# Attention blocks and product tiles of the later chunks moved to other steps, a few gate tiles' quadratic kept in PSUM

## The chip, the cores and the metric

The kernel runs on one core of one Trainium2 chip. The metric is the device time of one execution, in microseconds. Smaller is better.

## The reference

A gated linear attention feeds a network with a rational gate (the first network), and that feeds four experts (the second network). All data is float32.

```python
f = 1.0 / (1.0 + np.exp(-f_logit))              # B=4, H=8, S=768, D=48
for t in range(S):
    state = f[:, :, t, :, None] * state + np.einsum('bhd,bhe->bhde', k[:, :, t], v[:, :, t])
    y[:, :, t] = np.einsum('bhd,bhde->bhe', q[:, :, t], state)
x = y as (3072 tokens, 384)

h = x @ w_in                                    # 384 -> 2048
P = a[0] + a[1] * h + a[2] * h * h + a[3] * h * h * h
Q = 1.0 + np.abs(b[0]) * np.abs(h) + np.abs(b[1]) * h * h
x = (P / (Q + 1e-06)) @ w_out                   # 2048 -> 384

p = domain_probs / (domain_probs.sum(-1, keepdims=True) + 1e-09)
for e in range(4):
    out += p[:, e:e + 1] * (np.maximum(x @ w1[e], 0.0) @ w2[e])   # 384 -> 1024 -> 384
```

## The kernel before

**Chunks, tiles and steps.** The 768 positions are cut in six chunks of 128; a chunk holds 512 tokens (four batches). For a chunk, the first network has 16 tiles of 128 hidden units (`in1` is a tile's first product, its second product is part of an `out1`), and the second has 4 experts of 8 tiles (`in2`, `out2`). Every product of these tiles is split in three float32r products of a high and a low part (`wh`, `wl`, `gh`, `gl`), nine matmuls of 128x512 for an `in1`, `in2` or `out2`. One expert tile is one step `v`, 192 in all, so a chunk of the second network lasts 32 steps. While chunk c - 1 goes through the second network in steps 32(c - 1) to 32c - 1, chunk c goes through the attention and the first network in between. Chunk 0 has the first network to itself ahead of step 0: the "fill", with plain float32 products (`fill_in`, `fill_out`) and a time `tau = v + 19`.

**The order of the products** is written out in `first_mix_steps` and `product_order`. In a step, TensorE makes `in2` of the next tile, `out2` of the last one, and where the list `at` names the step, one `in1`. The list `ends` names four steps at which four finished first-network tiles are multiplied with their second weights at once (a "group", `out1`, 36 matmuls). A group uses the same three PSUM banks `acc` as `out2`, so `evac2` (L1018) first empties them: VectorE multiplies by the probabilities into `t`, GpSimd adds `t` to `o` (L1019). `evac1` (L1034, L1036) empties the group's sums. At a group's step the next `in2` is made early. The weights come in the order in which the list uses them, 14 halves ahead on SyncE's queue. A first use (all within steps -1 to 32) is split by ScalarE (L819) and GpSimd (L820) and stored; later uses load the split form.

**The gate** of a tile (`gate_in`, `gate_step`) takes two steps. ScalarE copies `h` out of the bank and makes `q` (the square), `r` and `y` (L929 to L935); VectorE makes the polynomials and one Newton step in `q` (L944 to L958, L968, L970), ScalarE and VectorE the two parts `gh` (L960) and `gl` (L975). `relu(v)` does the same for the second network (L983, L984). Engines take their instructions in program order: a step's relu stands ahead of its gate, the evacuation behind.

**The attention** of a chunk has four blocks (one per batch). `Att.t0` gives a block's offset, and `Att.stage` says what it does in steps 1 to 6 behind it: (1) `exp`, `w` (L431), four `scans` (L438); (2) `inverse` on ScalarE, `k_hat` on GpSimd (L452), `newton1` (L457), `newton2` (L462); (3) `q_hat` on GpSimd (L467); (4) scores (L471) and `masked` (L482); (5) transposed keys and outputs (`keys_and_y`, L487, L495), `k_copy`, `x_hi`; (6) state products (L538), `x_lo` (L552), `finish` (L564, L565). `PA`, `PB`, `ACT0`, `DVE1`, `REST` are places within a step: within `in2`, within `out2`, ahead of the gate on ScalarE, behind the gate on VectorE, and at the step's end. Each block's loads of f, k, q and v are issued on SyncE's queue in steps -1, 0 and 2. Blocks of chunks 2 and later keep some of their data in banks 6 and 7; those of chunk 1 use banks 5 to 7.

**Write-out.** When a chunk is through the second network, `write_out` transposes it by batch (L1043), ScalarE copies it to one of two buffers (L1050), and SyncE sends it out (L1052). `warm` (L608) makes 128x128 products that nobody reads.

Of the kernel before, what the change touches and what calls it, by code (L numbers as in the profile page):

```python
# [24 lines left out]
NJ1 = 16  # L25
# [320 lines left out]
def first_mix_steps():  # L346
# [3 lines left out]
    for c in range(1, NCH):  # L350
        p = NE * NJ2 * (c - 1)
        if c == 1:
            at = [10, 11, 12, 13, 14, 15, 16, 17, 18, 19, 20, 21, 23, 24, 25, 26]
            ends = (16, 20, 24, 29)
        else:
            at = [2, 3, 4, 5] if c == 2 else [-1, 1, 3, 5]
            at += [7, 9, 11, 13, 15, 17, 19, 21, 23, 24, 25, 26]
            ends = (8, 16, 24, 29)
        for j, s in enumerate(at):
            when[p + s] = (c, j)  # L360
        for n, s in enumerate(ends):
            groups[p + s] = (c, n)
# [205 lines left out]
class Att:  # L568
# [17 lines left out]
    def t0(c, b):  # L586
        if c == 1:
            return -6 + 3 * b
        if c == 2:
            return (8, 14, 20, 26)[b]  # L590
        return NE * NJ2 * (c - 1) - (30, 24, 17, 9)[b]
# [86 lines left out]
    def stage(self, blk, k):  # L678
        rs = range(NP)
        if k == 1:  # L680
# [8 lines left out]
        if k == 5:  # L689
            copy = [] if blk.last else [blk.k_copy]  # L690
            return {PB: 5 * idle + [blk.keys_and_y] + 3 * idle, REST: copy + [blk.x_hi]}
        if k == 6:
# [4 lines left out]
    def begin(self, v):  # L697
        ops = tuple([] for _ in range(7))
        for c in range(1, NCH):
            for b in reversed(range(NB)):  # L700
                k = v - self.t0(c, b)
# [7 lines left out]
def fused(ctx, tc, aps, consts, gm, big, dp, prep, flag_op):  # L709
# [215 lines left out]
    def gate_in(u):  # L925
        h = u[2]
        if u[0]:
            h = gp.tile([128, 512], F32, tag="h", name="h")
            nc.scalar.copy(out=h, in_=u[2])  # L929
        q = gp.tile([128, 512], F32, tag="q", name="q", bufs=3) if u[0] else banks[5 + u[1] % 2]  # L930
        r = gp.tile([128, 512], F32, tag="r", name="r")
# [133 lines left out]
    for v in range(-FILL - 6, LAST + 1):  # L1065
# [33 lines left out]
        if v in (LAST - 4, LAST - 3):  # L1099
            for b in range(2):  # L1100
                write_out(NCH - 1, b + 2 * (v - LAST + 4), banks[6 + b])
        if 0 <= c < NCH - 1 and k == 2:
            for b in range(2):
                write_out(c, b + (2 if c else 0), banks[6 + b])
        fill_run(ops[PB], 9 * any(item[0] == "out2" for item in items), True)
# [5 lines left out]
        for item in items[lead:]:  # L1111
            if item[0] == "in2":
                emit(item)
                if v + 1 < LAST:
                    relu(v + 1)
        if 0 <= c < NCH - 1 and k == (1 if c else 2):
            for b in range(2):
                write_out(c, b + (0 if c else 2), banks[6 + b])
        for item in items[lead:]:
# [8 lines left out]
        if tau == -1:  # L1128
            spread_probs()
        if 0 <= tau - 2 < NJ1:  # L1130
            fill_out(tau - 2)
# [198 lines left out]
```

## Time and profile before

| | |
|---|---|
| median of 3 runs | 1368.79 us (1368.64 to 1369.47) |
| the profiled execution | 1367.35 us |
| its span, first to last instruction | 1365.5 us |
| TensorE busy | 1325.7 us (97%) |
| VectorE busy | 870.5 us (64%) |
| ScalarE busy | 663.1 us (49%) |
| GpSimd busy | 287.6 us (21%) |
| mean granted TensorE clock | 0.993 |

All rows come from the profiled execution, so a sum is made against its span and then set beside the median. In the rows PE is TensorE, DVE VectorE, ACT ScalarE, POOL GpSimd, SP SyncE; L984 is line 984 of the kernel; `gl<-bank,gh` names what is written and what is read, and the name behind an arrow in a wait is what the wait ended with. [...]

### The profile page before, as it was taken

The page shows a single profiled execution, that of the slowest core. Times are in us where ns is not written, and L with a number is a line of the kernel's source. Part 1 is how long each engine was busy: PE and PEld are TensorE (multiplying, and loading weights), DVE is VectorE, ACT ScalarE, POOL GpSimd, SP SyncE. Part 2 cuts the span into 40 slices and gives each one's busy share as a digit, 9 for nine tenths or more (in the row PEclk, how much of TensorE's full clock was granted, in tenths as well). Part 3 has the DMA queues.
Part 4 walks back from the last instruction along what each step waited for, and adds up shares of the span by engine and source line. Part 5 has one row for each costly group of instructions (what it writes and reads, how often), then busy time and mean ns, then how long its engine had stood idle before and what let it go on. Part 6 is the DMA issues. An engine that isn't in the chain of part 4 may idle for free.

```text
span 1365.5 us, 19581 instructions
## 1 busy us (share of the span) xinstructions
PE 1325.7 (97%) x7152; PEld 1060.7 (78%) x7152; DVE 870.5 (64%) x1367; ACT 663.1 (49%) x1152; POOL 287.6 (21%) x257
## 2 busy tenths in 40 slices
PE   7899999898899999999999999999999999999998
PEld 6444788777788888888888888888888888888887
DVE  7999659677748576757666757576575465552221
ACT  3897448666536545525545535553445453431111
POOL 0133555566420020120110111001111000111010
PEclk9999999999999999999999999999999999999999
DMA  8547877667875666667656758665657676667660
GB/s 298 199 174 260 284 259 263 223 242 254 301 255 176 207 219 189 188 207 228 221 166 204 227 166 267 198 208 186 216 176 243 191 196 195 192 192 239 195 195 28
DMA packets 115706, 291.03 MB, mean 213 GB/s; under 512 B 13105, under 2 KB 28817, under 8 KB 114833
## 3 DMA queue, kind: packets, MB, share of 16 engines
q1 hardware_dynamic: 115024, 289.51, 65.9%
q8 instruction: 59, 0.97, 0.3%
q14 instruction: 47, 0.38, 0.1%
q10 hardware_dynamic: 576, 0.18, 0.1%
HBM read 240.83 MB, written 48.81 MB: 212 GB/s over the span
## 4 chain that ended last, share of the span: by engine, by line


## 5 line engine op out<-in xcount | busy, mean ns | idle before, releaser
L863 PE MATMUL bank<-x,w 128*128 128x512 f32 x2448 | 595.1, 391 | 6.7 <-DVE gl L984 6.7
L863 PEld LDWEIGHTS bank<-x,w 128*128 128x128 f32 x2448 | 457.2, 188 | 103.9 <-DVE gl L984 8.8
L873 PE MATMUL bank<-gh,w 128*128 128x512 f32 x1584 | 495.0, 394 | 6.6 <-DVE t L1018 6.6
L873 PEld LDWEIGHTS bank<-gh,w 128*128 128x128 f32 x1584 | 295.5, 189 | 73.2 <-DVE t L1018 7.9
L873 PE MATMUL bank<-gl,w 128*128 128x512 f32 x792 | 309.8, 391 | 0.0
L984 DVE SCALAR_TENSOR_TENSOR gl<-bank,gh 128x512 fp32r<-128x512 f32 x192 | 131.4, 685 | 154.5 <-ACT gh L983 154.2
L1019 POOL TENSOR_TENSOR o<-o,t 128x512 f32<-128x512 f32 x69 | 88.9, 1317 | 529.1 <-DVE t L1018 529.1
L873 PEld LDWEIGHTS bank<-gl,w 128*128 128x128 f32 x792 | 149.3, 189 | 31.3
L983 ACT ACTIVATE gh<-bank 128x512 fp32r<-128x512 f32 x192 | 113.7, 593 | 122.6 <-PE bank L863 122.6
L949 DVE SCALAR_TENSOR_TENSOR q<-q,sc,r 128x512 f32<-128x512 f32 x80 | 61.6, 770 | 141.8 <-ACT r L934 141.8
L960 ACT CAST gh<-q 128x512 fp32r<-128x512 f32 x80 | 49.2, 615 | 186.7 <-DVE q L958 186.6
L820 POOL TENSOR_TENSOR w<-rawbuf,w 128x384 fp32r<-128x384 f32 x96 | 104.5, 1113 | 88.6 <-ACT w L819 74.2
L929 ACT COPY h<-bank 128x512 f32<-128x512 f32 x80 | 46.8, 585 | 114.6 <-PE bank L863 113.9
L1036 DVE TENSOR_TENSOR s<-s,bank 128x512 f32<-128x512 f32 x45 | 31.0, 688 | 84.5 <-PE bank L873 84.4
L975 DVE TENSOR_TENSOR gl<-q,gh 128x512 fp32r<-128x512 f32 x80 | 55.9, 699 | 33.8 <-ACT gh L960 33.6
L950 ACT ACTIVATE r<-q,sc 128x512 f32<-128x512 f32 x80 | 58.0, 725 | 25.1 <-DVE q L949 18.4
L944 DVE SCALAR_TENSOR_TENSOR q<-q,r 128x512 f32<-128x512 f32 x80 | 69.5, 868 | 0.1
L935 ACT ACTIVATE y<-h,sc 128x512 f32<-128x512 f32 x80 | 64.2, 803 | 0.0
L958 DVE SCALAR_TENSOR_TENSOR q<-y,sc,q 128x512 f32<-128x512 f32 x80 | 62.2, 778 | 1.8
L970 DVE SCALAR_TENSOR_TENSOR y<-y,sc,h 128x512 f32<-128x512 f32 x80 | 61.1, 764 | 2.8
L951 ACT ACTIVATE r<-r 128x512 f32<-128x512 f32 x96 | 60.7, 633 | 3.0
L968 DVE TENSOR_TENSOR y<-y,h 128x512 f32<-128x512 f32 x80 | 57.2, 716 | 0.0
(113 smaller groups left out, 1220.5 us busy)
## 6 DMA issues: line engine op xcount, KB each, us to landing
w<-ws SPq DMA_DIRECT2D x448, 384.0 KB, 3.6
ws<-w SPq DMA_DIRECT2D x96, 384.0 KB, 4.1
raw<-in_w_dram SPq DMA_DIRECT2D x16, 768.0 KB, 6.3
rawbuf<-in_w_dram SPq DMA_DIRECT2D x64, 192.0 KB, 3.9
v<-in_v_dram SPq DMA_DIRECT2D x24, 320.0 KB, 4.8
f<-in_qkf_dram SPq DMA_DIRECT2D x24, 256.0 KB, 4.0
k<-in_qkf_dram SPq DMA_DIRECT2D x24, 256.0 KB, 4.3
q<-in_qkf_dram SPq DMA_DIRECT2D x24, 256.0 KB, 4.6
```

Source lines behind the costliest of these rows:

```text
L820: nc.gpsimd.tensor_tensor(out=t[:, 1], in0=r, in1=t[:, 0].bitcast(F32), op=ALU.subtract)
L863: nc.tensor.matmul(ps, a[:, o], b[:, kk, :], start=(n == 0), stop=(n == 8))
L873: nc.tensor.matmul(acc[m], a[:, o], b, start=(start and n == 0), stop=(stop and n == last))
L935: nc.scalar.activation(out=y, in_=h, func=AF.Identity, scale=sc[:, 0:1], bias=sc[:, 1:2])
L944: vec.scalar_tensor_tensor(out=q0, in0=q0, scalar=QC, in1=r0, op0=ALU.add, op1=ALU.mult)
L949: vec.scalar_tensor_tensor(out=q, in0=q, scalar=sc[:, 5:6], in1=r, op0=ALU.mult, op1=ALU.add)
L951: nc.scalar.activation(out=r, in_=r, func=AF.Exp, scale=-1.0)
L958: vec.scalar_tensor_tensor(out=q0, in0=y0, scalar=sc[:, 3:4], in1=q0, op0=ALU.subtract, op1=ALU.mult)
L970: vec.scalar_tensor_tensor(out=y, in0=y, scalar=sc[:, 2:3], in1=h, op0=ALU.subtract, op1=ALU.mult)
L983: nc.scalar.activation(out=gh, in_=h, func=AF.Relu)
L984: nc.vector.scalar_tensor_tensor(out=gl, in0=h, scalar=0.0, in1=gh.bitcast(F32), op0=ALU.max, op1=ALU.subtract)
L1019: nc.gpsimd.tensor_tensor(out=o[c][:, m], in0=o[c][:, m], in1=t, op=ALU.add)
```

## The change

Five things change together. (1) Chunk 2's first-network tiles and groups take chunk 1's pattern (one tile per step from the eleventh step on), and chunk 3's first two tiles come two steps and one step later. (2) The blocks of chunk 2 start at offsets 20, 25, 30, 35 instead of 8, 14, 20, 26, and those of chunk 3 at 42, 47, 52, 57 instead of 34, 40, 47, 55; a block's last step then falls together with the next one's first, and `begin` takes the older block first. (3) The first block of chunk 1 does its first three stages a step later, with `q_hat` in the same step as `newton2`, its scores at the step's end and `masked` in the next step; ten `warm` products are put ahead of the fill's last but one `fill_out`. (4) `q` of tiles 0 to 8 of chunk 1 lies in bank 6 or 7 instead of SBUF. (5) Chunk 0's write-out uses bank 5, one batch at a time over two steps; that of chunks 1 to 4 is made wholly in its third step instead of its second and third.

```diff
--- before.py
+++ after.py
@@ -349,11 +349,11 @@
     when, groups = {}, {}
     for c in range(1, NCH):
         p = NE * NJ2 * (c - 1)
-        if c == 1:
+        if c < 3:
             at = [10, 11, 12, 13, 14, 15, 16, 17, 18, 19, 20, 21, 23, 24, 25, 26]
             ends = (16, 20, 24, 29)
         else:
-            at = [2, 3, 4, 5] if c == 2 else [-1, 1, 3, 5]
+            at = [1, 2, 3, 5] if c == 3 else [-1, 1, 3, 5]
             at += [7, 9, 11, 13, 15, 17, 19, 21, 23, 24, 25, 26]
             ends = (8, 16, 24, 29)
         for j, s in enumerate(at):
@@ -587,7 +587,9 @@
         if c == 1:
             return -6 + 3 * b
         if c == 2:
-            return (8, 14, 20, 26)[b]
+            return 20 + 5 * b
+        if c == 3:
+            return 42 + 5 * b
         return NE * NJ2 * (c - 1) - (30, 24, 17, 9)[b]
 
     def start(self, fetch):
@@ -676,7 +678,10 @@
                     self.blocks[c, b].load_v()
 
     def stage(self, blk, k):
-        rs = range(NP)
+        if blk.c == 1 and blk.b == 0 and k < 5:
+            return ({}, {ACT0: [blk.exp], DVE1: [blk.w], REST: [blk.scans]},
+                    {ACT0: [blk.inverse], POOL1: [blk.k_hat], DVE1: [blk.newton1], REST: [blk.newton2, blk.q_hat]},
+                    {REST: [blk.all_scores]})[k - 1]
         if k == 1:
             return {ACT0: [blk.exp], DVE1: [blk.w], REST: [blk.scans]}
         if k == 2:
@@ -688,7 +693,8 @@
         idle = [lambda: None]
         if k == 5:
             copy = [] if blk.last else [blk.k_copy]
-            return {PB: 5 * idle + [blk.keys_and_y] + 3 * idle, REST: copy + [blk.x_hi]}
+            first = [blk.masked] if blk.c == 1 and blk.b == 0 else []
+            return {DVE1: first, PB: 5 * idle + [blk.keys_and_y] + 3 * idle, REST: copy + [blk.x_hi]}
         if k == 6:
             upd = [] if blk.last else 4 * idle + [blk.all_updates] + 4 * idle
             return {PA: upd, DVE1: [blk.x_lo], REST: [] if blk.last else [blk.finish]}
@@ -697,7 +703,7 @@
     def begin(self, v):
         ops = tuple([] for _ in range(7))
         for c in range(1, NCH):
-            for b in reversed(range(NB)):
+            for b in reversed(range(NB)) if c == 1 else range(NB):
                 k = v - self.t0(c, b)
                 if 1 <= k <= 6:
                     for at, fs in self.stage(self.blocks[c, b], k).items():
@@ -927,7 +933,7 @@
         if u[0]:
             h = gp.tile([128, 512], F32, tag="h", name="h")
             nc.scalar.copy(out=h, in_=u[2])
-        q = gp.tile([128, 512], F32, tag="q", name="q", bufs=3) if u[0] else banks[5 + u[1] % 2]
+        q = gp.tile([128, 512], F32, tag="q", name="q", bufs=3) if u[0] > 1 or u[0] and u[1] > 8 else banks[5 + u[0] + u[1] % 2]
         r = gp.tile([128, 512], F32, tag="r", name="r")
         y = gp.tile([128, 512], F32, tag="y", name="y")
         nc.scalar.activation(out=q, in_=h, func=AF.Square)
@@ -1099,9 +1105,11 @@
         if v in (LAST - 4, LAST - 3):
             for b in range(2):
                 write_out(NCH - 1, b + 2 * (v - LAST + 4), banks[6 + b])
-        if 0 <= c < NCH - 1 and k == 2:
+        if c == 0 and k in (2, 3):
+            write_out(c, 2 * k - 4, h1)
+        if 0 < c < NCH - 1 and k == 2:
             for b in range(2):
-                write_out(c, b + (2 if c else 0), banks[6 + b])
+                write_out(c, b, banks[6 + b])
         fill_run(ops[PB], 9 * any(item[0] == "out2" for item in items), True)
         for item in items[lead:]:
             if item[0] == "out2":
@@ -1113,9 +1121,11 @@
                 emit(item)
                 if v + 1 < LAST:
                     relu(v + 1)
-        if 0 <= c < NCH - 1 and k == (1 if c else 2):
+        if c == 0 and k in (2, 3):
+            write_out(c, 2 * k - 3, h1)
+        if 0 < c < NCH - 1 and k == 2:
             for b in range(2):
-                write_out(c, b + (0 if c else 2), banks[6 + b])
+                write_out(c, b + 2, banks[6 + b])
         for item in items[lead:]:
             if item[0] == "out1":
                 emit(item)
@@ -1127,6 +1137,8 @@
                 gate[u[:2]] = gate_in(u)
         if tau == -1:
             spread_probs()
+        if tau == NJ1:
+            att.warm(10)
         if 0 <= tau - 2 < NJ1:
             fill_out(tau - 2)
         for f in ops[REST]:
```

## Rows read from the trace of the kernel before

**Rows 1.** Stretches of the span: length, each engine's busy time (instructions), granted clock, DMA.

```profile
234.10:262.80 28.70, 24.46 (x97) 19.73 (x97) 18.15 (x28) 16.83 (x33) 18.63 (x17) 0.88 0.60 202
262.80:294.10 31.30, 30.39 (x199) 24.74 (x198) 23.89 (x36) 22.03 (x43) 17.45 (x17) 1.00 0.65 229
294.10:322.80 28.70, 24.11 (x114) 18.43 (x112) 23.93 (x35) 19.51 (x35) 15.44 (x15) 1.00 0.85 301
...
340.00:376.00 36.00, 32.41 (x157) 26.04 (x155) 28.81 (x44) 19.08 (x36) 18.12 (x17) 1.00 0.87 301
376.00:561.00 185.00, 184.49 (x1067) 152.18 (x1066) 116.59 (x187) 88.43 (x150) 26.77 (x26) 1.00 0.66 209
```

**Rows 2.** TensorE's waits from 136 to 376 us: total, times, longest.

```profile
PE bank L863 <- DVE gl L984: 6.7, 5, 2.5
PE bank L873 <- DVE t L1018: 6.6, 3, 4.2
```

**Rows 3.** Stretches behind two waits, the clock as share of full speed.

```profile
242.80:249.70 6.90, 5.49 (x13) 4.39 (x14) 6.15 (x10) 2.31 (x6) 5.47 (x4) 0.51 0.00 1
...
126.00:130.20 4.20, 4.20 (x6) 1.35 (x6) 4.05 (x8) 0.63 (x1) 1.28 (x1) 0.59 1.05 400
```

**Rows 4.** TensorE's waits from 376 to 1270 us.

```profile
PE bank L1043 <- POOL o L1019: 2.2, 3, 0.8
```

**Rows 5.** VectorE's timeline ahead of step 16's evacuation: start, length, instruction.

```profile
225.43 0.55 DVE L552 TENSOR_TENSOR x<-bank,x 128x384 fp32r<-128x384 f32 x1
226.50 0.73 DVE L564 TENSOR_TENSOR am<-bank,s 48x192 f32<-48x192 f32 x2
...
235.06 1.35 DVE L438 TENSOR_TENSOR_SCAN g<-bank,sc 112x128 f32<-112x128 f32 x4
```

**Rows 6.** VectorE's groups from 195 to 345 us: count, busy us, mean ns, idle before.

```profile
L946 DVE SCALAR_TENSOR_TENSOR q<-q,r 128x512 f32<-128x512 f32 x13 | 14.1, 1085 | 0.4
L944 DVE SCALAR_TENSOR_TENSOR q<-q,r 128x512 f32<-128x512 f32 x14 | 13.8, 982 | 0.0
```

**Rows 7.** VectorE's groups from 400 to 1240 us.

```profile
L958 DVE SCALAR_TENSOR_TENSOR q<-y,sc,q 128x512 f32<-128x512 f32 x64 | 48.0, 751 | 1.7
...
L946 DVE SCALAR_TENSOR_TENSOR q<-q,r 128x512 f32<-128x512 f32 x15 | 10.4, 692 | 0.5
```

**Rows 8.** Groups of the whole span: the same product with a bank.

```profile
L944 DVE SCALAR_TENSOR_TENSOR bank<-bank,r 128x512 f32<-128x512 f32 x16 | 11.1, 692 | 0.1
```

**Rows 9.** GpSimd's groups from 195 to 345 us.

```profile
L820 POOL TENSOR_TENSOR w<-rawbuf,w 128x384 fp32r<-128x384 f32 x59 | 65.0, 1126 | 43.7 <-ACT w L819 38.4 <-DMA ws<-w 4.9
```

**Rows 10.** VectorE's groups from 294.1 to 322.8 us.

```profile
L944 DVE SCALAR_TENSOR_TENSOR q<-q,r 128x512 f32<-128x512 f32 x3 | 4.0, 1340 | 0.0
L958 DVE SCALAR_TENSOR_TENSOR q<-y,sc,q 128x512 f32<-128x512 f32 x3 | 3.0, 999 | 0.0
```

**Rows 11.** VectorE's groups from 340 to 362.7 us.

```profile
L944 DVE SCALAR_TENSOR_TENSOR q<-q,r 128x512 f32<-128x512 f32 x3 | 3.1, 1049 | 0.0
...
L946 DVE SCALAR_TENSOR_TENSOR q<-q,r 128x512 f32<-128x512 f32 x2 | 2.1, 1043 | 0.1
```

**Rows 12.** Timeline around chunk 0's write-out; in brackets the idle time before.

```profile
391.81 2.21 PE L863 MATMUL bank<-x,w 128*128 128x512 f32 x9
...
393.86 0.82 PE L1043 MATMUL bank<-ident,o 128*128 128x128 f32 x6
...
399.69 0.95 ACT L1050 COPY os<-bank 128x384 f32<-128x384 f32 x2 [4.45 <-DMA out_dram<-os]
...
401.18 0.69 DVE L984 SCALAR_TENSOR_TENSOR gl<-bank,gh 128x512 fp32r<-128x512 f32 x1 [9.89 <-ACT gh L983]
```

**Rows 13.** Timeline at the fill's end.

```profile
125.85 4.54 PE L920 MATMUL bank<-g,wf 128*128 128x512 f32 x6 [2.65 <-DVE g L963]
...
131.71 1.26 DVE L482 TENSOR_TENSOR am<-bank,mask 128x512 f32<-128x512 f32 x2
...
136.52 1.70 DVE L457 SCALAR_TENSOR_TENSOR i<-g,r 112x512 f32<-112x512 f32 x1 [0.92 <-ACT r L447]
```

## The prediction

> **What bounds the kernel now.** I read the stretches first [rows 1]: each row gives a stretch's length and TensorE's busy time in it, and the difference is what TensorE stood still. From 376 to 561 us (steps 31 to 57, where chunk 2 goes through the first network) it is 185.00 - 184.49 = 0.5 us, so there TensorE sets the pace and nothing beside it matters. Ahead of that it is 4.24, 0.91, 4.59 and 3.59 us, 13.3 us in all, in the steps in which the first network's chunk 1 runs (10 to 29). All of this change's possible gain inside the steps lies there. The waits [rows 2] say for whom TensorE stood: DVE's `t` (the evacuation ahead of a group, 6.6 us in 3 waits) and DVE's `gl` of the relu (6.7 us in 5). So in steps 10 to 29 VectorE is the bound at places, although its mean load is low: it comes late at the group's evacuation and two steps behind a group. [...] Behind 400 us TensorE waits at three write-outs for GpSimd's sum `o`, 2.2 us [rows 4].
>
> **The first dense stretch (steps 10 to 20).** The diff takes chunk 2's attention out of steps 9 to 20 (it starts with step 21) and puts the gate's `q` of tiles 0 to 8 in PSUM. What that removes from VectorE just ahead of the 4.24 us wait is in its timeline [rows 5]: one `x_lo` 0.55, one `finish` 0.73, four scans 1.35, 2.6 us, with four products of the same blocks around them. The PSUM tiles: here `q*r` with both inputs in SBUF takes 0.98 and 1.09 us [rows 6], in the later chunks the second of them takes 0.69 [rows 7], and with `q` in a bank the first takes 0.69 in the fill [rows 8]. The difference is GpSimd's 59 splits of 1.13 us [rows 9], which run in this stretch and in none behind 400 us. So a tile gains 0.29 + 0.39 = 0.7 us of VectorE, and the five tiles between steps 11 and 16 gain 3.4 us. Together 6.0 us, against a lateness of 4.24: the evacuation at step 16 is in time. I leave 0.3 us of wait, because behind the evacuation's place in VectorE's queue stand the gate's nine instructions, which begin with ScalarE's reading of a product that TensorE has only just made. If the wait goes, the clock has no reason to fall: the waits for `gl`, up to 2.5 us [rows 2], were not followed by a fall, while 4.24 and the fill's 2.65 were. That is -3.9 - 3.4 = -7.3 us. Bounds: 0 (the cause is another) and -7.6. At step 20 the 0.91 us wait stood behind one more `x_lo`, which goes: -0.45 (0 to -0.9).
>
> What a bank costs VectorE is a place to weigh. The fill's row with a bank says 0.692, the quiet SBUF row says 0.692 [rows 7, 8]: no price.
> [...]
>
> **The rest of chunk 1 (steps 21 to 29) stays.** Block 0 of chunk 2 now starts where block 2 did (offset 20), so steps 21 to 26 hold the same attention work, and tiles 9 to 15 keep `q` in SBUF. The 4.59 us recur, less the GpSimd product of the `finish` that is gone at step 20, which frees about one doubled instruction: -0.7. Block 1 has its first two steps at 26 and 27 (block 3 had them at 27 and 28); VectorE has the same sum of work after, so the 3.59 us recur: 0. Bounds: -3.5 if a head start carries over, +1 if `x_lo`, `finish`, `w` and scans in one step 26 come at a worse time.
>
> **Steps 30 to 41** now hold blocks 2 and 3 and no first-network tiles. VectorE has its relu (0.69 [rows 12]) and 6 us of attention spread over 5 steps of 4 us; TensorE hides it. If the cover failed a block's masked product would be late by its two instructions, 1.3 us. The loads move with their blocks: four a block, all on SyncE's queue among the weights. Their buffers are double, and the block before last is done in each case, so SyncE does not stand longer in front of the weights; count and bytes are the same. Chunk 2's 32 weight halves are read some eight steps later, 14 ahead of use as before: 0.
>
> **The second dense stretch (steps 42 to 61) is the price.** Chunk 2's tiles now run one per step, as chunk 1's do, with chunk 3's blocks 0 to 3 beside them, and with `q` in SBUF. Today this chunk loses 0.5 us. After, it repeats chunk 1's pattern without the splits, so I take chunk 1's waits and remove what the splits made of them. Step 48: 0.9, the twin of 0.91 with its `x_lo` at the same place. Steps 53 to 56: the twin of 4.59, less the excess of the slowed instructions over their quiet rows [rows 7, 10]: 3 x (1.34 - 0.69) for L944 and 3 x (1.00 - 0.75) for L958, 2.7; plus block 1's last step, which falls on step 53 (0.55 + 0.73): 3.2. Steps 57 to 61: the twin of 3.59, less 3 x (1.05 - 0.69) and 2 x (1.04 - 0.69) [rows 11], 1.8: 1.8. Sum +5.9. Bounds: +1 and +16.7 (all that chunk 1 loses, its clock too). The sixth evacuation of the pattern adds three VectorE and three GpSimd instructions where TensorE has 36 products of a group (four times 2.05 us [rows 12]): 0.
>
> **Write-outs.** For chunks 1 to 4 all four transposes move to the step behind, where GpSimd's sums are done: the three waits go, -2.2. In exchange ScalarE copies four times in one step through two buffers and waits for the first output transfers. Today chunk 0 does so: 4.45 us [rows 12], and nothing shows on TensorE. ScalarE's queue then holds the next relu; its `gl` began 7.3 us behind the first transpose and took 0.7, 8.0. TensorE asks for it after two sets of transposes (0.82 each) and three times nine products (2.05 from start to start): 7.8. So 0.2 to 0.3 us are lost in chunk 4, where no first-network product lengthens the step. Sum -1.9 (bounds -2.2 and +1, if the transfers land late in all four). Chunk 0's four go through bank 5 one at a time in light steps: 0.
>
> **The fill's end.** Block 0 of chunk 1 starts a step later, so its `w` and scans no longer stand in front of the gate of tile 14, whose product waited 2.65 us and then ran at half clock for most of its 4.54 [rows 13]. The ten warming products fill what is left of that wait (bank 4 is free by then). By the transposes' row, six products of their shape in 0.82 us [rows 12], they take 1.4 us, which they would cost if no wait were left. But VectorE has next to no pause there (4.05 of 4.20 us busy [rows 3]); the same instructions are only put in another order. The fill can end sooner by no more than the wait, 2.65 us. Against that, `masked` (1.26), which stood ahead of the splits of the fill's result, now stands behind block 1's `newton1` (1.70 here, with a GpSimd product beside it [rows 13]), and the block's outputs on TensorE wait for both in series: 2.96 - 2.65 = 0.3. I take +0.3; bounds -1.5 (everything gained stays) and +1.
>
> **The sum.** -7.3 - 0.45 - 0.7 + 5.9 - 1.9 + 0.3 = -4.15 us. The profiled execution took 1367.35 us, 1.85 more than its span of 1365.5: 1363.2 for one like it, and 1364.6 against the median of 1368.79. Within 0.2% (2.7 us) is about what a measurement of this kernel cannot tell from no change.
>
> **Rivals.** *Clean*: without splits VectorE keeps up in chunk 2 (cost 1 instead of 5.9), and a head start halves the rest of chunk 1's waits (3.5 less): 1356.2. For it: from 400 us on, four tiles in successive steps with a block's scans between them cost TensorE nothing. Against it: those had one block, not three.
> *Moved, not removed*: VectorE comes to step 48 as late as it came to step 16, and chunk 2 loses all 16.7 us that chunk 1 loses, clock included, instead of 5.9: 1375.4, slower. It decides at a lateness over some 2.6 us at 48 or 52, from where the clock has fallen today. For it: the same tiles beside the same blocks. Against it: 59 splits are missing.
> *Not attention at all*: ScalarE, with its share of the splits, holds up the gate and so the evacuation; step 16 keeps wait and clock: 1371.9. Against it: none of VectorE's rows ahead of that wait [rows 5] has a pause in front, so it was late by its own work.
> *The bank's price*: a bank source costs VectorE what it spares it, the five tiles gain nothing, and of the 4.24 us 1.6 stay (4.24 - 2.6), too short for the fall: 1365.9. Against it: the pair of 0.692.
>
> **Numbers.** Forecast 0.47, clean 0.20, moved 0.14, not attention 0.14, bank 0.05. The likeliest gives 1364.6, its own range 1360.5 to 1368.5. With 1355.5 to 1372.5, the moved burst (0.14) and the lower part of the clean case (0.06) stay outside. Faster: 0.36 of the forecast's 0.47, all of clean, half of bank, 0.58; slower: moved and parts of the others, 0.19; same 0.23.
>
> **What would show it.** In the profile after: no wait of over 1 us for `t` and full clock in steps 16 and 17; waits for `gl` in steps 22 to 29 as today; 3 to 6 us of waits for DVE in chunk 2's steps 48 to 61; no wait for `o` at the write-outs; no fall of the clock at the fill's end. Wrong: a fall of the clock in chunk 2, or chunk 1's 8 us gone.

## The result and the profile after

The changed kernel is slower: 1377.27 us (median of 6 runs, 1374.77 to 1378.44) against 1368.72 (1366.13 to 1369.47), a ratio of 1.0064 with a 95% interval of 1.0053 to 1.0076. The forecast was 1364.6, its range ended at 1372.5. The profiled execution took 1377.28 us, its span is 1375.4, 9.9 more than before. In the changed file the lines behind the new `stage` are 6 further down (L984 is L990, L1018 is L1024, L1043 is L1049).

First, where the time came from. The starts of the relus (ScalarE's `gh`, L983 and L989) mark the steps in both traces. Relu 0 starts at 139.72 before and 141.01 after (+1.3, the fill); relu 64 at 597.82 and 602.76 (so +3.7 in steps 0 to 63, where the forecast had -2.55); relu 191 at 1353.07 and 1362.54 (+4.5 in steps 64 to 191, where it had -1.9). The rest, 0.4, lies behind relu 191.

TensorE's waits from 136 to 376 us and from 376 to 1270 us, in the changed kernel (total, times, longest):

```profile
PE bank L869 <- DVE gl L990: 6.7, 2, 4.7
PE bank L879 <- DVE t L1024: 3.3, 3, 2.1
...
PE bank L869 <- DVE gl L990: 6.4, 8, 1.9
PE bank L1049 <- ACT os L1056: 1.9, 2, 1.0
PE bank L879 <- DVE t L1024: 1.0, 2, 0.8
```

Against [rows 2, 4]: the waits for `t` are halved and none is 4.2 long; those for `gl` have the same total, but one of 4.7 us where the longest was 2.5; behind 376 us there is 9.3 us where there was 2.2, the waits for `o` are gone, and waits for ScalarE's copies `os` are new.

The stretches of the same kernel, cut at the starts of steps 16, 22, 30 and 42 and at 255, 315 and 590 us, and the one of the long fall of the clock (length; busy us of TensorE, its weight loads, VectorE, ScalarE, GpSimd; granted clock; DMA):

```profile
230.90:255.00 24.10, 23.45 (x104) 19.10 (x103) 13.44 (x21) 17.11 (x34) 15.85 (x16) 1.00 0.64 227
255.00:288.40 33.40, 31.31 (x138) 25.55 (x138) 24.87 (x38) 24.53 (x47) 18.69 (x18) 1.00 0.78 267
288.40:315.00 26.60, 23.96 (x108) 18.85 (x107) 21.34 (x32) 17.32 (x34) 16.65 (x15) 0.94 0.74 263
315.00:350.70 35.70, 31.04 (x185) 24.93 (x186) 29.80 (x41) 21.78 (x41) 19.36 (x19) 0.90 0.86 302
350.70:422.40 71.70, 71.70 (x516) 59.03 (x515) 32.43 (x59) 17.45 (x35) 19.06 (x20) 1.00 0.72 234
422.40:590.00 167.60, 163.10 (x911) 132.72 (x910) 125.64 (x200) 91.57 (x154) 29.76 (x27) 0.99 0.62 194
343.80:350.60 6.80, 4.70 (x13) 3.37 (x15) 5.61 (x8) 1.84 (x5) 3.60 (x4) 0.50 0.66 232
```

Length less TensorE's busy time is its idle time: 0.65 us at step 16 (4.24 before [rows 1]), 2.09 at step 20 (0.91), 2.64 in steps 22 to 25 (4.59), 4.66 in 26 to 29 (3.59), none in 30 to 41, and 4.5 in the second dense stretch (0.51). The clock moved too. The fall behind step 16 [rows 3] is gone; a new one of 6.8 us stands in step 28 (the last row, 0.50 of full speed), and shorter ones, 3.4 us each at 0.51 and 0.50, begin at 299.4 and 579.3. At the lower clock nine products take 4.21 us instead of 2.2 (below), so TensorE loses half of the time that it is busy in a fall. The start of a fall can lie in the end of the wait before it (343.80, and the wait ends at 345.90): TensorE is busy for 4.70 of the last row's 6.80 us, so 2.35 are lost, and for 5.49 of the 6.90 in [rows 3], so 2.7 and not 3.4. In the two short ones TensorE is busy throughout, 1.7 lost in each.

**Steps 26 to 28** hold the new long wait. The changed kernel's timeline there (start, length, engine, line; in brackets the idle time before):

```profile
331.57 0.55 DVE L552 TENSOR_TENSOR x<-bank,x 128x384 fp32r<-128x384 f32 x1
332.15 0.69 DVE L431 TENSOR_SCALAR bank<-f 112x512 f32<-112x512 f32 x1
332.76 0.68 DVE L981 TENSOR_TENSOR gl<-q,gh 128x512 fp32r<-128x512 f32 x1
333.36 0.73 DVE L564 TENSOR_TENSOR am<-bank,s 48x192 f32<-48x192 f32 x2
...
334.12 1.36 DVE L438 TENSOR_TENSOR_SCAN g<-bank,sc 112x128 f32<-112x128 f32 x4
...
335.99 1.50 DVE L950 SCALAR_TENSOR_TENSOR q<-q,r 128x512 f32<-128x512 f32 x1
...
337.52 1.39 DVE L952 SCALAR_TENSOR_TENSOR q<-q,r 128x512 f32<-128x512 f32 x1
338.84 1.77 DVE L955 SCALAR_TENSOR_TENSOR q<-q,sc,r 128x512 f32<-128x512 f32 x1
...
345.17 0.68 DVE L990 SCALAR_TENSOR_TENSOR gl<-bank,gh 128x512 fp32r<-128x512 f32 x1
...
345.90 4.21 PE L869 MATMUL bank<-x,w 128*128 128x512 f32 x9 [4.66 <-DVE gl L990]
```

Block 0's last step (`x_lo` L552, `finish` L564) and block 1's first (`w` L431, scans L438) are both in step 26, 3.33 us of VectorE in one place, and the next gate's products then take 1.50, 1.39 and 1.77 us. TensorE waits 4.66 us for the `gl` two relus later, and its nine products then take 4.21 us at the lower clock, where they take 2.2 elsewhere.

**A write-out** in the changed kernel, chunk 2's at step 98:

```profile
836.11 0.82 PE L1049 MATMUL bank<-ident,o 128*128 128x128 f32 x6
836.12 0.63 ACT L939 ACTIVATE q<-h 128x512 f32<-128x512 f32 x1
...
839.48 0.84 ACT L1056 COPY os<-bank 128x384 f32<-128x384 f32 x2
...
839.99 0.93 PE L1049 MATMUL bank<-ident,o 128*128 128x128 f32 x6 [0.97 <-ACT os L1056]
...
841.99 0.48 ACT L1056 COPY os<-bank 128x384 f32<-128x384 f32 x1 [1.67 <-DMA out_dram<-os]
...
845.29 0.48 ACT L1056 COPY os<-bank 128x384 f32<-128x384 f32 x1 [2.83 <-DMA out_dram<-os]
845.67 0.60 ACT L989 ACTIVATE gh<-bank 128x512 fp32r<-128x512 f32 x1
...
852.40 2.33 PE L869 MATMUL bank<-x,w 128*128 128x512 f32 x9 [0.97 <-DVE gl L990]
```

The copies stand behind a tile's gate on ScalarE, so the first comes 3.4 us after the transposes began; the second pair of transposes waits for the copies (0.97), the last two copies wait for the transfers of the first two (1.67 and 2.83), and the next relu behind them is late (845.67). VectorE then works through its queue without a pause, and TensorE meets the lateness one relu further on, at 852.40. The four transfers, 192 KB each, took 1.9, 4.8, 4.1 and 1.9 us to land here. The profiled executions of two kernels with the same write-out (chunk 2's blocks apart, no warming products, both below) have no such wait at that relu. From relu 95 to relu 127 it takes 211.3 us before, 213.7 here, and 211.8 and 211.6 in those two.

### The profile page after: what moved, and what is told of

Read it like the earlier page. It is cut to its first block, busy times and chain, and to the rows that moved or that the text cites. A ratio compares the mean times of both kernels' runs of the same rounds, so it can differ in the third digit from the quotient of the medians.

```text
span 1375.4 us, 19637 instructions
## 1 busy us (share of the span) xinstructions
PE 1331.7 (97%) x7172; PEld 1063.6 (77%) x7172; DVE 861.5 (63%) x1370; ACT 661.7 (48%) x1152; POOL 284.6 (21%) x260
## 4 chain that ended last, share of the span: by engine, by line
## 5 line engine op out<-in xcount | busy, mean ns | idle before, releaser
L869 PE MATMUL bank<-x,w 128*128 128x512 f32 x2448 | 600.7, 393 | 13.3 <-DVE gl L990 13.1
L990 DVE SCALAR_TENSOR_TENSOR gl<-bank,gh 128x512 fp32r<-128x512 f32 x192 | 131.4, 685 | 174.2 <-ACT gh L989 174.0
L1025 POOL TENSOR_TENSOR o<-o,t 128x512 f32<-128x512 f32 x72 | 91.9, 1306 | 518.3 <-DVE t L1024 518.3
L989 ACT ACTIVATE gh<-bank 128x512 fp32r<-128x512 f32 x192 | 113.7, 594 | 150.0 <-PE bank L869 150.0
L955 DVE SCALAR_TENSOR_TENSOR q<-q,sc,r 128x512 f32<-128x512 f32 x71 | 54.4, 767 | 117.2 <-ACT r L940 117.2
L826 POOL TENSOR_TENSOR w<-rawbuf,w 128x384 fp32r<-128x384 f32 x96 | 99.9, 1070 | 92.3 <-ACT w L825 78.5
L966 ACT CAST gh<-q 128x512 fp32r<-128x512 f32 x71 | 43.6, 614 | 156.1 <-DVE q L964 156.1
L981 DVE TENSOR_TENSOR gl<-q,gh 128x512 fp32r<-128x512 f32 x71 | 48.9, 689 | 30.0 <-ACT gh L966 29.9
L950 DVE SCALAR_TENSOR_TENSOR q<-q,r 128x512 f32<-128x512 f32 x71 | 64.1, 902 | 0.0
L956 ACT ACTIVATE r<-q,sc 128x512 f32<-128x512 f32 x71 | 51.5, 725 | 22.1 <-DVE q L955 15.8
L1024 DVE TENSOR_TENSOR t<-bank,pb 128x512 f32<-128x512 f32 x72 | 46.8, 685 | 19.0 <-PE bank L879 18.9
```

Source lines behind the costliest of these rows:

```text
L826: nc.gpsimd.tensor_tensor(out=t[:, 1], in0=r, in1=t[:, 0].bitcast(F32), op=ALU.subtract)
L869: nc.tensor.matmul(ps, a[:, o], b[:, kk, :], start=(n == 0), stop=(n == 8))
L950: vec.scalar_tensor_tensor(out=q0, in0=q0, scalar=QC, in1=r0, op0=ALU.add, op1=ALU.mult)
L955: vec.scalar_tensor_tensor(out=q, in0=q, scalar=sc[:, 5:6], in1=r, op0=ALU.mult, op1=ALU.add)
L989: nc.scalar.activation(out=gh, in_=h, func=AF.Relu)
L990: nc.vector.scalar_tensor_tensor(out=gl, in0=h, scalar=0.0, in1=gh.bitcast(F32), op0=ALU.max, op1=ALU.subtract)
```

## The experiments

Each kernel ran next to the kernel before on the same chip, and its ratio is to that. A difference from the changed kernel is the difference of two such ratios times 1368 us; each ratio's interval is 0.1 to 0.2% to either side (1.2 to 2.7 us), so such a difference is good to some 2 us.

**Chunk 2's blocks apart**, the changed kernel with one number line changed:

```diff
-            return 20 + 5 * b
+            return (20, 26, 31, 36)[b]
```

> The changed kernel, with chunk 2's blocks at offsets 20, 26, 31, 36 instead of 20, 25, 30, 35, so that in chunk 1's dense steps no block's last step shares a step with the next one's first. Theory (the shared step 26 makes one wait of 4.66 us out of the 2.47 and 1.11 of before, and that one is long enough to be followed by a fall of the clock): the waits in steps 26 to 30 come back to about 3.6 us in two, no fall of the clock behind them, 4.5 us faster than the changed kernel, about 1373. Rival (VectorE's sum of work decides there, however it is spread): same waits, same time, 1377.

1372.3 us, 1.0028 (1.0019 to 1.0036): 4.9 less than the changed kernel. Its waits from 136 to 376 us:

```profile
PE bank L869 <- DVE gl L990: 4.9, 3, 2.5
PE bank L879 <- DVE t L1024: 4.3, 3, 2.1
```

The 4.66 us wait is one of 2.47, as before. It is 4.66 or 4.67 in the changed kernel and in the four kernels below that keep the shared step (write-outs as before, chunk 3's tiles, no warming, `q` in SBUF), and 2.46 or 2.47 in the three that do not have it (this one and the two put together at the end). So the shared step is what makes the long wait. What it costs is less than the 4.9: from TensorE's first `out2` product for relu 27 to that for relu 32 it takes 37.2 us before, 40.1 in the changed kernel, 39.5 in the four others with the shared step and 37.2 to 37.4 in the three without, so 2.3 to 2.9 us. The fall behind the wait is 6.8 us long in the changed kernel's profiled execution only, and 3.4 in the four others; one of 3.4 stands behind the wait of 2.47 here too, where the theory had none. The two profiled executions differ by another 2.9 us from relu 64 to relu 191, at write-outs whose code is the same in both.

**Write-outs of chunks 1 to 4 as before**, the changed kernel with that edit undone:

```diff
         if 0 < c < NCH - 1 and k == 2:
             for b in range(2):
-                write_out(c, b, banks[6 + b])
+                write_out(c, b + 2, banks[6 + b])
...
-        if 0 < c < NCH - 1 and k == 2:
+        if 0 < c < NCH - 1 and k == 1:
             for b in range(2):
-                write_out(c, b + 2, banks[6 + b])
+                write_out(c, b, banks[6 + b])
```

> The changed kernel, with the write-outs of chunks 1 to 4 made as before (two batches at the end of their second step, two in the third). Theory (four copies through two buffers in one step make TensorE wait for ScalarE's copy and then for the relu's gl, 3.3 us in five waits, against 2.2 us in three of before): 1 us faster, 1376, with waits of 0.7 us for GpSimd's o in their place. Rival, as the prediction had it (the move spares 1.9 us): 2 us slower, 1379.

1371.87 us, 1.003 (1.002 to 1.0041): 4.7 less, where 1 was expected. Waits from 376 to 1270 us:

```profile
PE bank L869 <- DVE gl L990: 3.5, 3, 1.9
PE bank L1049 <- POOL o L1025: 1.4, 2, 0.8
PE bank L879 <- DVE t L1024: 1.0, 2, 0.8
```

The two waits for `os` (1.9) and five of the eight for `gl` (2.9) go, two for `o` (1.4) come back. The waits of 0.20 and 1.32 at chunk 3's first tiles (steps 68 and 69) go as well, so those came of the write-out that ran into these tiles. From relu 64 to relu 191 it takes 755.3 us before, 754.3 in this kernel, 759.8 in the changed one, and 756.9, 757.2 and 758.2 in three more that have its write-outs and tiles there (blocks apart, no warming, `q` in SBUF). So the write-outs cost 2.6 to 5.5 us against the old ones, and the changed kernel's profiled execution is the worst of them.

**Chunk 3's first tiles where they were**, and **no warming products**, each alone in the changed kernel:

```diff
-            at = [1, 2, 3, 5] if c == 3 else [-1, 1, 3, 5]
+            at = [-1, 1, 3, 5]
```

> The changed kernel, with chunk 3's first two tiles at the steps of before (63 and 65 instead of 65 and 66). Theory (three tiles in successive steps beside the first block of chunk 4 make the two waits for gl of 1.5 us at steps 68 and 69): they go, 1.5 us faster, 1375.8. Rival (the tile at 63 meets block 3's last step, and its wait comes there): same time, 1377.

```diff
-        if tau == NJ1:
-            att.warm(10)
```

> The changed kernel without the ten warming products. Theory (TensorE waits there for VectorE's gate in any case, and a wait of 2.65 us was followed by a fall of the clock): the wait for tile 14's or 15's gate grows by the products' time, the clock falls at the fill's end, the fill ends about as late: 0 to 1.7 us slower, 1377 to 1379. Rival (the products push the fill's end, since they take over 2 us and the wait is shorter): 1 to 2 us faster, 1375.5.

1375.67 (1.0056, 1.0043 to 1.0069) and 1374.57 (1.0051, 1.0038 to 1.0064). Neither can be told from the changed kernel. In the first kernel the waits of steps 68 and 69 give way to one of 1.00 for `os`. In the second the fill's end has waits of 1.34 and 1.75 and, without any warming, no fall of the clock either.

**`q` of all chunk 1's tiles in SBUF again**, the rest of the change kept:

```diff
-        q = ... if u[0] > 1 or u[0] and u[1] > 8 else banks[5 + u[0] + u[1] % 2]
+        q = ... if u[0] else banks[5 + u[1] % 2]
```

> The changed kernel with the gate's q of all tiles of chunk 1 in SBUF again. Theory (the split products on GpSimd slow VectorE's products of two SBUF inputs by some 0.7 us a tile, and this had half the part in the wait at step 16): the wait ahead of step 16's group comes back to 2 us or more, perhaps with a fall of the clock, and the one at step 20 grows: 2 to 5 us slower than the changed kernel, 1379 to 1382. Rival (taking the attention out of steps 9 to 20 was enough, ScalarE sets the pace there): the same 0.7 and 2.1 us, 1377.

1386.29 us, 1.0121 (1.0101 to 1.014), 7.8 more than the changed kernel and more than either side expected. With no attention in steps 10 to 20, step 16 still waits 0.45 and 3.66 us and the clock falls for 6.8 us; step 20 waits 3.65. TensorE's wait for the group's `t` at step 16, in the kernel before, in this one and in the changed one:

```profile
244.21 0.80 PE L873 MATMUL bank<-gh,w 128*128 128x512 f32 x1 [4.24 <-DVE t L1018]
```

```profile
241.41 0.79 PE L879 MATMUL bank<-gh,w 128*128 128x512 f32 x1 [3.66 <-DVE t L1024]
```

```profile
237.46 0.50 PE L879 MATMUL bank<-gh,w 128*128 128x512 f32 x1 [0.65 <-DVE t L1024]
```

Counted from the start of relu 10 (190.73, 192.21 and 192.01), the wait ends at 53.48, 49.20 and 45.45 us, and TensorE begins it at 49.24, 45.54 and 44.79. So without the attention VectorE is 4.3 us earlier, but TensorE is earlier by nearly as much, since the attention's own products on TensorE left the same steps (4.4 us of its time from the `out2` of relu 10 to that of relu 15). With `q` in PSUM as well VectorE is another 3.75 us earlier, and TensorE has nothing less to do.

VectorE's products there, first the changed kernel's and then this one's (195 to 238 us; count, busy us, mean ns, idle before):

```profile
L952 DVE SCALAR_TENSOR_TENSOR bank<-bank,r 128x512 f32<-128x512 f32 x5 | 3.5, 700 | 0.2
```

```profile
L952 DVE SCALAR_TENSOR_TENSOR q<-q,r 128x512 f32<-128x512 f32 x5 | 7.0, 1392 | 0.2
L955 DVE SCALAR_TENSOR_TENSOR q<-q,sc,r 128x512 f32<-128x512 f32 x6 | 4.4, 741 | 4.7 <-ACT r L940 4.7
L990 DVE SCALAR_TENSOR_TENSOR gl<-bank,gh 128x512 fp32r<-128x512 f32 x6 | 4.2, 692 | 9.3 <-ACT gh L989 9.3
```

VectorE has pauses, 9.3 us for the relu's `gh` and 4.7 for the gate's `r` (3.6 and 1.9 in the kernel before), and is late all the same: its work and ScalarE's run in turns. In the timeline one step lasts 7.15 us here (a relu's `gl` starts at 227.51, the next at 234.66) and 6.32 in the changed kernel (225.16, 231.48), while TensorE's own products of a step take 6.12. The slowed product stands in that chain.

**Only the dense tiles of chunk 2**, in the kernel before (its attention unmoved):

```diff
-        if c == 1:
+        if c < 3:
...
-            at = [2, 3, 4, 5] if c == 2 else [-1, 1, 3, 5]
+            at = [-1, 1, 3, 5]
```

> The kernel before with one thing changed: chunk 2's tiles and groups in chunk 1's pattern, one tile a step, its attention and all else as before. Theory (the density itself is the price of the second dense stretch, as the prediction had it, since the gate and the blocks of chunk 3 are then in the same steps): 4 to 6 us of waits for VectorE in steps 48 to 61, 1373 to 1374. Rival (what costs time is where the blocks of chunk 3 now lie): under 1 us of waits there, 1369.

1368.58 us, 1.0004 (0.9995 to 1.0013). From 376 to 1270 us it waits 0.98 us for `gl` and 0.7 for `t` beside the 2.2 for `o`. One tile per step does not cost by itself. Three of chunk 3's blocks lie among the dense tiles here too; in the changed kernel all four do, and steps 48, 53 and 58 hold the last step of one block and the first of the next. Which of these costs how much was not tested alone.

**Chunk 2's later blocks two steps on**, in the kernel before:

```diff
-            return (8, 14, 20, 26)[b]
+            return (8, 16, 22, 28)[b]
```

> The kernel before with one thing changed: chunk 2's blocks 1 to 3 start two steps later (16, 22, 28 instead of 14, 20, 26), so that block 1's scans and products lie behind the group of step 16 and not in front of it. Theory (the wait of 4.24 us is made by the block's VectorE work in the steps just ahead of the evacuation, and the clock's fall follows it): that wait shrinks below 2 us, no fall behind it, 5 to 7 us faster than before, 1362 to 1364, if the later blocks do no more harm at steps 20 to 30 than they do today. Rival (the lateness is made by the splits and comes with any block near a group): a wait of 2 to 4 us at step 20 or 24 in its place, the same 1368.

1366.99 us, 0.999 (0.9981 to 0.9999). In this kernel the last block's `finish` reads a bank that the write-out has already used, so the state of chunk 3 is another one; the work is the same. Step 16 waits 2.00 instead of 4.24, and then step 20 waits 3.62 and step 24 3.51: the wait for `t` moved to the next groups (9.1 us in 3 waits, 6.6 before).

**The fill's part alone**, in the kernel before:

```diff
+        if blk.c == 1 and blk.b == 0 and k < 5:
+            return (...)
...
+        if tau == NJ1:
+            att.warm(10)
```

> The kernel before with the fill end's part of the change alone: block 0 of the second chunk begins a step later and ten warming products stand at the fill's end. Theory: the fill's end is 0.5 to 1 us later, as in the changed kernel, and the clock fall of 3.4 us at 126.8 stays away (1.7 back), so 1367.5 to 1369 us, no difference that can be told. Rival (the first block a step later and the warming cost the time by themselves): 1370 to 1372 us.

1368.08 us, 0.9998 (0.9989 to 1.0007). The clock fall at the fill's end is gone and relu 0 starts at 140.2, 0.5 later than before.

**GpSimd's subtraction replaced by a fill of zeros**, in the kernel before:

```diff
-                nc.gpsimd.tensor_tensor(out=t[:, 1], in0=r, in1=t[:, 0].bitcast(F32), op=ALU.subtract)
+                nc.gpsimd.memset(t[:, 1].bitcast(F32), 0.0)
```

> The kernel before with GpSimd's subtraction (L820, two SBUF operands, one result) replaced by a fill of zeros of the same tile: the low part of the weights is left out of the computation, the number of GpSimd instructions and the products on TensorE stay. Theory (the splits on GpSimd slow VectorE's products of two SBUF operands from 692 to 944 and 1085 ns in the dense stretch, and that is what makes chunk 1's steps wait): L944 and L946 fall to 0.69 to 0.75 us in steps 8 to 31, the waits of steps 16 to 30 (13.3 us idle and two to three clock falls) shrink to under 5 us, 1357 to 1362 us in all. Rival (VectorE's queue and its chain with ScalarE set the waits, the engine's slowness beside GpSimd is small change): waits within 3 us of before, 1366 to 1369 us.

1359.37 us, 0.9943 (0.9929 to 0.9956). VectorE's and GpSimd's groups from 195 to 345 us:

```profile
L944 DVE SCALAR_TENSOR_TENSOR q<-q,r 128x512 f32<-128x512 f32 x15 | 12.6, 839 | 0.0
...
L946 DVE SCALAR_TENSOR_TENSOR q<-q,r 128x512 f32<-128x512 f32 x14 | 10.7, 762 | 0.5
...
L820 POOL MEMSET w<- 128x384 f32 x62 | 23.5, 420 | 12.0 <-PE bank L863 6.6 <-ACT r L951 3.2 <-PE bank L873 1.6
```

Against [rows 6, 9], L946 falls from 1085 to 762 ns and L944 only from 982 to 839 (the theory had 690 to 750 for both, and under 5 us of waits). TensorE's waits for `t` and `gl` from 136 to 376 us go from 13.3 [rows 2] to 7.0 us, and the fall at step 16 from 6.8 to 3.4. So the splits make about half of these waits. The fill of zeros is also shorter than the subtraction (420 against 1126 ns). So one more kernel has three of them for each subtraction, and keeps GpSimd busy as long, with nothing to read:

> As the kernel with one fill of zeros, but with three of them in place of each of GpSimd's subtractions: at 420 ns each GpSimd is busy 1.26 us a tile, more than with the subtraction (1.13), and reads nothing; the low part of the weights is left out. Theory (VectorE's products of two SBUF tensors wait for a GpSimd instruction that reads SBUF): L946 stays at 0.70 to 0.80 us and L944 near 0.84, the waits from 136 to 376 us stay at 7 to 8 us, 1358 to 1362 us. Rival (it is GpSimd being busy, or late with its splits): L946 near 1.09 us, waits near 13 us, 1366 to 1369 us.

1359.68 us, 0.9938 (0.9924 to 0.9952). VectorE's two products (two lines further down: L946 is L944, L948 is L946) and one of the three fills, from 195 to 345 us:

```profile
L946 DVE SCALAR_TENSOR_TENSOR q<-q,r 128x512 f32<-128x512 f32 x15 | 12.9, 860 | 0.0
...
L948 DVE SCALAR_TENSOR_TENSOR q<-q,r 128x512 f32<-128x512 f32 x14 | 10.7, 762 | 0.5
...
L821 POOL MEMSET w<- 128x384 f32 x62 | 26.0, 419 | 3.6
```

GpSimd spends 77.6 us on them, more than on the splits (65.0 [rows 9]), and waits, products and time are those of the single fill. So it is not GpSimd's being busy that slows VectorE's products and makes half of chunk 1's waits. What is left is its reading, or the length of one instruction (1126 ns against 419), which no run here tells apart. The fills also start without ScalarE's copy of the high part, for which the splits wait (38.4 us of GpSimd's idle time in [rows 9]). The waits alone do not separate that from the other two; the products' times fell as well, which no late split explains: from 195 to 238 us the product of L946 (L952 in the changed file) took 1392 ns beside the splits (`q` in SBUF again), 700 with a bank (the changed kernel) and 692 beside the single fills.

**What pointed ahead**: two kernels put together. The first is the changed kernel with the blocks of chunk 2 as in the first experiment, those of chunk 3 at 42, 47, 53 and 58, chunk 3's tiles at 0, 1, 3 and 5, the write-outs of chunks 1 to 4 as before and no warming.

> The changed kernel with every part put right that cost time: chunk 2's blocks at 20, 26, 31, 36, chunk 3's at 42, 47, 53, 58 and its first two tiles at steps 64 and 65, write-outs of chunks 1 to 4 as before, no warming products. Theory (the parts' costs add up: 4.9 + 4.6 + 1 + 1.8 us): 1365, some 3 us faster than the kernel before. Rival (the waits are one lateness of VectorE that only changes its place): 1369 or more, no faster than before.

1367.5 us, 0.9993 (0.9984 to 1.0002), between the theory's 1365 and the rival's 1369. The second has no shared step at all, `q` in PSUM only for tiles 4 to 8 of chunk 1, and the fill's end of the kernel before; here is its difference from the changed kernel in the blocks and `q`:

```diff
-            return 20 + 5 * b
+            return (8, 20, 26, 32)[b]
-            return 42 + 5 * b
+            return 38 + 6 * b
-        q = ... if u[0] > 1 or u[0] and u[1] > 8 else banks[...]
+        q = ... if u[0] > 1 or u[0] and not 4 <= u[1] <= 8 else banks[...]
```

> Chunk 2's blocks begin after steps 8, 20, 26 and 32, chunk 3's after 38, 44, 50 and 56, so that no first step lies on another block's last one; q lies in PSUM for tiles 4 to 8 of chunk 1 alone; write-outs, fill end and warming as before. Theory (the price of the change is the place of the blocks and of the write-outs, its gain is step 16 without a block): the 4.24 us wait of step 16 and its clock fall stay away (-7), step 20 costs about 2 instead of 0.91 (+1), the waits of the rest of chunk 1 are those of c2_apart without the shared step (0.36, 1.49, 2.5), chunk 3's blocks under dense tiles cost 1 to 2: 1361 to 1365 us. Rival (whatever leaves chunk 1's VectorE-bound steps comes back at full price later): 1367 to 1370 us, as the kernel before.

1370.59 us, 1.0014 (1.0005 to 1.0023). Its waits from 376 to 1270 us:

```profile
PE bank L874 <- DVE t L1019: 3.8, 2, 2.8
PE bank L1044 <- POOL o L1020: 1.4, 2, 0.7
PE bank L864 <- ACT h L930: 0.9, 1, 0.9
```

Step 16 waits 0.60 and step 20 2.10, but chunk 2's groups at steps 48 and 52 now wait 1.02 and 2.77 for `t`. The theory of 1361 to 1365 fell; the rival, in which the saving comes back in the other stretch (1367 to 1370), is borne out.

## Why the prediction was wrong, step by step

**Step 16: near in size, by two errors that cancelled.** -7.3 was forecast. The wait went from 4.24 to 0.65 and the fall behind it went too: -3.6 and -2.7, so -6.3. (No run shows the 3.4 us that the forecast put on the fall: TensorE waited for 1.4 of the 6.90 us at 0.51 anyway and was busy for 5.49 [rows 3], and half of that, 2.7, was lost.) VectorE's timeline ahead of the wait has three short pauses for ScalarE's `r` (0.2 to 0.6 us), where the forecast read none. The working set 6.0 us of VectorE's work against a lateness of 4.24 us. VectorE's `t` came 8.0 us earlier, more than that; but TensorE came 4.45 us earlier too, because the attention that leaves takes its TensorE products with it, which the working left out. So the 2.6 us for the attention gained 0.1 us of wait (4.11 of the 4.24 us stay with `q` in SBUF), and the 3.4 us for the five tiles' `q` (3.75 measured) made the gain. That the wait came out near the 0.3 us forecast is luck. The rival of the bank's price (1.6 stay) is wrong: the product takes 700 ns with a bank and 1392 with SBUF, and the gate's other four products with `q` take 684 to 752 ns with a bank and 689 to 741 with SBUF. That the attention had to leave for it is another thing: its later blocks use banks 6 and 7.

**Step 20: the wrong sign.** -0.45 was forecast, +1.2 came (2.09 against 0.91), with the same `x_lo` gone. The step that failed is the same: one engine's work was counted. The moved block's products on TensorE lay in steps 18 to 20, 3.25 us from the `out2` of relu 17 to that of relu 19. Where they still are (the kernel before, the dense tiles alone, the fill's part alone) the wait is 0.87 to 0.91; where steps 18 and 19 have none, it is 2.09 to 2.11 with `q` in PSUM and 3.62 and 3.65 with `q` in SBUF.

**"The rest of chunk 1 stays" is the first failed step that cost much.** For steps 26 to 29 the forecast was 0, on the ground that VectorE's sum of work is the same, with +1 if the four parts meet in step 26. They met: +1.1 of idle and 2.35 of the clock, +3.4 in the profiled execution, and 2.3 in the four others with the shared step. Taking the shared step apart brings the wait back to 2.47. The sum over a stretch was the wrong measure; what counted here is the longest burst in one step, because a relu stands behind it in VectorE's queue and the products of that step meet GpSimd's splits (1.50, 1.39 and 1.77 us above). For steps 21 to 25 -0.7 was forecast, -0.25 came.

**"Sum -1.9" for the write-outs is the second and largest, with the wrong sign.** Undoing the edit gave 4.7 us back (good to 2), and steps 64 to 191 grew by 4.5 in the profiled execution. The working took chunk 0's write-out as the model, in a step that has no gate; in chunks 1 to 3 the copies stand behind a gate, and the transposes behind the copies, and chunk 3's first tiles come on top (1.52 us in steps 68 and 69, forecast nowhere). The waits for `o` did go, as said; another wait took their place.

**The premise on the clock was wrong as well, but it is not what made the kernel slower.** Waits up to 2.5 us were taken to leave the clock alone. In the kernel with chunk 2's blocks apart it fell at a wait of 2.11 and at the one of 2.47, and in the changed kernel at 2.06 and 1.86, the last of these in chunk 2: the forecast's own "Wrong: a fall of the clock in chunk 2". But falls behind the waits of chunk 1 are nothing new. The kernel with the fill's part alone runs the code of the kernel before in those steps, and its clock fell behind the same two waits, 2.08 and 2.47. The first fall cost it nothing, as the same 71 matmuls show, before and then there (the third column from the right is the clock); behind the second it is 0.1 us later.

```profile
304.36:322.80 18.44, 14.53 (x71) 10.84 (x71) 15.05 (x21) 13.06 (x24) 7.51 (x8) 1.00 0.79 282
```

```profile
304.47:322.91 18.44, 15.74 (x71) 12.03 (x71) 15.04 (x21) 13.06 (x25) 7.51 (x8) 0.91 0.78 277
```

TensorE is slower and waits less for VectorE, which sets the pace there. The same holds for the changed kernel's fall at 299.4, whose 1.7 us stand against 1.95 less of idle. The profiled execution of the kernel before is also a rare one: its mean granted clock is 0.993, 75 of the 77 executions of it beside the experiments have 0.988 to 0.992, and the changed kernel's six have 0.989 to 0.991.

**The second dense stretch: right in size, not in cause.** +5.9 was forecast, and 4.0 of idle and 1.7 of the clock came, 5.7. But chunk 1's pattern of tiles alone costs nothing that can be told (0.9995 to 1.0013), so the size is luck: what is left as the cause is the place of the blocks, of chunk 3's above all. The forecast's twin at step 48 (0.9) was 0.23. The wait that begins at 534.2 (1.41) is for a relu's `gl` behind a gate and two products of a block in VectorE's queue, and that gate's first product took 1.46 us at 527.67 beside `k_hat` on GpSimd, with 0.69 where nothing runs beside it.

**The fill's end:** +0.3 was forecast. Alone it moves relu 0 by 0.5 and the whole by nothing that can be told. In the changed kernel relu 0 is 1.3 later, part of it from a fall at 36.6 (3.4 us at 0.50; 1.00 there before) that comes and goes among kernels whose code there is the same.

Summed as measured: 1.3 (the fill) - 6.3 + 1.2 - 0.25 + 3.4 + 5.7 + 4.5 = 9.55, of the 9.9 by which the span grew; 0.4 lies behind relu 191. Between this and the forecast's -4.15 lie 14.1 us: 6.4 of them from the write-outs and chunk 3's first tiles, 3.4 from steps 26 to 29, 1.6 from step 20, 1.0 each from the fill and step 16. These are one execution of each kernel; the medians differ by 8.6. The forecast's range left out this side because the burst in step 26 had a bound of +1, the write-outs one of +1, and step 20 none above 0.

What stays open: why a wait of some 2 to 2.5 us is followed by a fall in one execution and not in another, what in the place of chunk 3's blocks costs the 5.7 us, and whether some place for chunk 2's and 3's blocks keeps step 16's gain. The first of the combined kernels and that of two steps' delay come out level with the kernel before or 0.1% under it; no kernel that does the whole computation was shown to be faster.

## What to carry to other kernels

A wait is the difference of two arrivals. When work is moved out of a stretch, count what it takes from both engines: the attention's leaving made VectorE 4.3 us earlier and TensorE nearly as much, and the wait 0.1 us shorter. Speeding up a product that only the late engine runs went into the wait in full (0.69 us in each of nine tiles: 7.8 us in all). When blocks are moved, lay out each step's burst on the engine that feeds the critical one, not the stretch's sum; two blocks that share step 26 cost 2.3 to 2.9 us here. And a model for a moved piece of work must come from a step with the same queue ahead of it. One profiled execution is one sample: the same write-out cost 2.5 us in one trace and 0.3 in another.

## What the hardware showed that was not expected

A product on VectorE of two SBUF tensors took double its time even where GpSimd was nearly idle: the second dense stretch has no splits (GpSimd is busy for 29.76 of its 167.60 us), and yet one such product took 1.38 us against 0.69, while `q_hat` ran (timeline of the changed kernel):

```profile
535.05 1.28 POOL L467 TENSOR_TENSOR q<-q,i 112x512 f32<-112x512 f32 x1 [6.47 <-DVE i L462]
535.49 1.38 DVE L950 SCALAR_TENSOR_TENSOR q<-q,r 128x512 f32<-128x512 f32 x1
```

The clock fell at waits of 1.86 to 2.11 us in the traces of several kernels here, but not at one of 2.47 us in the kernel before; behind one and the same wait of 4.66 to 4.67 us the fall was 6.8 us long in one trace and 3.4 in four. And where TensorE waited for VectorE again soon after (304 to 323 us), a fall of 3.4 us cost nothing: 18.44 us for the same 71 matmuls with it and without it.
